# Case: one total order of a fused RWKV-7 and SwiGLU kernel exchanged for another

## The chip, the cores and the metric

One NeuronCore of a Trainium2 chip runs the whole program. The time is device microseconds of one execution; of the kernel before three runs are shown, and their median stands for it. Five engines work side by side, each through its own queue in order: TensorE (PE in the profile, its weight loads PEld), VectorE (DVE), ScalarE (ACT), GpSimd (POOL) and SyncE (SP), which only issues transfers. An engine waits for another one through semaphores. The profile shows one execution: the span from the first to the last instruction, what each engine did in it, and the clock that was granted to TensorE.

## The reference, cut to what matters

The first half is a recurrence over 768 time steps with one 40x40 state for each of 4 x 8 heads; its output, 3072 tokens of 320 numbers, goes through an RMS norm and a gated feed-forward block with 1536 hidden units. The weights arrive as 64-bit floats.

```python
for t in range(S):                                   # S = 768
    y[:, :, t] = np.einsum('bhd,bhde->bhe', rt, state)
    Sa = np.einsum('bhde,bhe->bhd', state, at)
    state_decay = state * wt[:, :, None, :] - np.einsum('bhd,bhe->bhde', Sa, bt)
    state = state_decay + np.einsum('bhd,bhe->bhde', vt, kt)
...
rms = np.sqrt(np.mean(x * x, axis=-1, keepdims=True) + 1e-06)
xn = x / rms * rms_g                                 # x: 3072 x 320
g = xn @ w_gate                                      # 320 x 1536
silu = g * (1.0 / (1.0 + np.exp(-g)))
val = xn @ w_val
return (silu * val @ w_out).astype(np.float32)
```

## The kernel before

**Tiling.** The 768 steps are cut into 24 chunks of 32. Within a chunk the recurrence is written as matrix products, so that only the state passes from chunk to chunk. A chunk c has three stages in the code:

- `front(c)` loads the chunk's inputs with transfers, mostly from GpSimd's queue (`wan`, `kbn`, `wn`, `VU`), turns them with TensorE transposes ("turn"), builds products of decays level by level (levels 1, 2, 4, 8, 16) and forms Gram products ("gramk", 32 small products a piece on 64-row tiles); VectorE puts their results under masks into `LT`, a triangular matrix for each head. Four transfers each then take `LT` through DRAM into another layout (`sB`, then `M`) on SP's queue.
- `inverse(c)` inverts those triangular matrices on VectorE, row by row (`Yi`, `tmp`), and sends the result back through DRAM (`sY`, then `LT`), again on SP's queue.
- `main(c)` carries the state forward: "state" and "lower" products, ScalarE's scaled copy `Xs`, a second "lower" (the solve, which reads the inverse that has landed in `LT`), ScalarE's copies into `VU`, "update" and VectorE's addition into `ST`. It then forms the outputs ("score", masks into `As`, "level" and "y0" products, sums into `y`), normalizes them (`ss`, `x`) and lays them, turned ("turn4", "turn3"), as 128-token columns into `xg`.

`feed(g)` is the feed-forward block for one or two chunks (13 groups, the first and the last with one chunk). It goes through the 12 slices of 128 hidden units two at a time: "h64" (products on half the rows) and "hh" (four full 128x128 products with 256 columns) into one PSUM room, ScalarE's SiLU into `sg`, VectorE's product into `hT`, and "out" (128x320 products) summed in `po` over all slices; at the end ScalarE copies `po` to `o` and four transfers on SP's queue store it. Around feed 0 `narrow` turns the 64-bit weights into 32-bit ones on VectorE and ScalarE.

A matrix product of the code is two products and two weight loads in TensorE's stream, a transpose is one of each; a piece of 16 small matrix products thus takes 64 instructions, a piece of 32 takes 128.

**What sets the order.** No loop order reaches the engines. Each call above adds a *piece* (one or more instructions of one engine) to a `Plan` with its needs; 5993 pieces in all (VectorE 2717, ScalarE 1113, TensorE 1091, GpSimd 588, SyncE 484). `Plan.issue` then walks the list `ORDER` and issues one piece per number. A number is the distance from the first piece that isn't issued yet, so the list is one total order, and each engine's queue is that order cut to its pieces. PSUM is given out the same way: `po` has one pair of banks, and three further pairs are shared by 495 *rooms*, short-lived buffers. A room's pair is its digit in `PAIRS`, and a room is entered only when the earlier one on that pair has been left. Between pieces of different engines that touch different banks or quadrants of a pair `issue` declares that there is no dependence; all others on a pair are kept apart by semaphores.

The list may also hold the word "-", which would issue a product on the identity that nothing uses (`plan.warm`, into a part of `po`). In the list of this kernel that word doesn't occur. `WARM` and `warm_until` are stored and not read on.

In the profile most instructions have the line of the helper that recorded them: L486 is any VectorE piece, L509, L513 and L516 ScalarE's activations, copies and scalings, L529 all transfers, L532 matrix products, L535 transposes. Groups are told apart by their tiles: `ps` is any room, `po<-wf,hT` an "out" product, `ps<-xg,wf` "h64" or "hh", `ps<-Xs,LT` the solve, `ps<-VU,KN` an update.

```python
i = first + int(word)          # in Plan.issue: the next piece
gone.add(i)
while first in gone:
    first += 1
...
nc.scalar.copy(po_[:, 0, DM:DM + P], plan.pairs[0][:, 0, 0:P])   # ahead of all pieces
```

Of the kernel before, what the change touches and what calls it, by code (L numbers as in the profile page):

```python
# [7 lines left out]
FP32 = mybir.dt.float32  # L8
# [8 lines left out]
P = 128  # L17
# [7 lines left out]
WARM = 230.0  # L25
# [232 lines left out]
class Plan:  # L258
# [82 lines left out]
    def issue(self, order, pairs):  # L341
# [6 lines left out]
        for word in order.split():  # L348
            if word == "-":
                self.order.append(None)  # L350
                self.warm()
                continue
# [759 lines left out]
```

## Time and profile before

| | us |
|---|---|
| runs shown | 1023.4, 1028.79, 1029.04 |
| median | 1028.79 |
| span of the profiled execution | 1017.9 |
| TensorE busy | 928.0 (91%), 24512 products |
| TensorE's weight loads busy | 754.3 (74%), 24512 loads |
| VectorE busy | 779.5 (77%) |
| ScalarE busy | 510.6 (50%) |
| GpSimd busy | 343.2 (34%) |
| mean granted clock of TensorE | 0.953 of full |

For the profiled execution only its span is given; what lies around the span is seen from the runs, which are 5.5 to 11.1 us longer. In the profile's slices a digit is the busy share of a fortieth of the span in tenths; PEclk is the clock in the same way. In the rows of stretches each engine has its busy time and, in brackets, its instructions; the last three columns are the granted clock, the transfers' share and GB/s. A wait is written as who waited, then for whom, with the sum, the times and the longest. In the timeline a row has start, duration, engine, line, what was written from what, and how many instructions in a row; the brackets tell how long the engine sat idle before it and what ended that. "issue" means that the profile shows nothing that it waited for.

### The profile page before, as it was taken

To read this page: it belongs to the slowest core of one execution; us is meant where nothing else is said; L and a number is where in the kernel's file an instruction comes from. 1 tells how busy PE (TensorE), PEld (TensorE's weight loads), DVE (VectorE), ACT (ScalarE), POOL (GpSimd) and SP (SyncE) were. 2 spreads that over 40 slices of the span, in tenths; PEclk is the share of its full clock that TensorE was granted. 3 is DMA by queue.
4 is the path that set the end of the run, shared out by engine and by line. 5 is a ranking of instruction groups with operands and counts; after the bars stand their busy time and mean duration, and the time that the engine had idled before them with its cause. 6 is when DMAs were issued, how large, how long until landed. Compare 5 with 4: busy or idle time off the path is not lost.

```text
span 1017.9 us, 55372 instructions
## 1 busy us (share of the span) xinstructions
PE 928.0 (91%) x24512; PEld 754.3 (74%) x24512; DVE 779.5 (77%) x2718; ACT 510.6 (50%) x1134; POOL 343.2 (34%) x595
## 2 busy tenths in 40 slices
PE   3457779998999999999999999999999999999998
PEld 3446668877777777787877778777787787787776
DVE  9989987786967976967868779669688788776531
ACT  6878656544454544454463444544535545435131
POOL 9966543313233233224321433224233323400000
PEclk9657768999999999999999999999999999999999
DMA  7764543313333223233231242232322422420100
GB/s 170 159 178 109 124 91 78 74 32 69 52 67 63 51 60 75 43 67 68 48 75 32 61 88 48 50 70 45 70 58 46 78 48 60 76 45 9 45 6 20
DMA packets 140175, 68.87 MB, mean 68 GB/s; under 512 B 120768, under 2 KB 127264, under 8 KB 139936
## 3 DMA queue, kind: packets, MB, share of 16 engines
q0 software_dynamic: 19680, 32.48, 15.8%
q1 hardware_dynamic: 118080, 32.54, 15.2%
q8 instruction: 192, 3.15, 1.3%
q10 hardware_dynamic: 2176, 0.33, 0.2%
q14 instruction: 47, 0.39, 0.1%
HBM read 55.05 MB, written 10.22 MB: 64 GB/s over the span
## 4 chain that ended last, share of the span: by engine, by line
PE 71%; DVE 12%; issue 5%; DMA 5%; ACT 3%; SPq 3%; DVEq 0%; ACTq 0%
PE ps L532 50%; PE po L532 14%; PE ps L535 6%; SPq L529 3%; DVE Yi L486 3%; DMA sY<-Yi 2%; DVE tmp L486 2%; DVE As L486 1%; DVE y L486 1%; ACT VU L513 1%; DVE LT L486 1%; DMA sB<-LT 1%; DVE K L486 1%; DVE wf L486 1%; DMA LT<-sY 1%
## 5 line engine op out<-in xcount | busy, mean ns | idle before, releaser
L532 PE MATMUL ps<-xg,wf 128*128 128x256 f32 (+3 forms) x1872 | 360.5, 374 | 2.4 <-issue 1.6
L532 PEld LDWEIGHTS ps<-xg,wf 128*128 128x128 f32 (+1 forms) x1872 | 267.5, 189 | 50.6 <-issue 14.5
L532 PE MATMUL po<-wf,hT 128*128 128x320 f32 x576 | 180.5, 447 | 0.5 <-issue 0.5
L486 DVE TENSOR_TENSOR hT<-ps,sg 128x256 f32<-128x256 f32 (+1 forms) x156 | 59.9, 399 | 95.3 <-PE ps L532 53.7
L532 PEld LDWEIGHTS po<-wf,hT 128*128 128x128 f32 x576 | 102.6, 189 | 37.8 <-issue 3.7
L486 DVE TENSOR_TENSOR tmp<-Yi,M 128x24 f32<-128x24 f32 (+21 forms) x512 | 107.3, 210 | 12.2 <-DMA M<-sB 1.4
L486 DVE TENSOR_TENSOR Yi<-Yi,tmp 128x24 f32<-128x24 f32 (+21 forms) x512 | 107.1, 209 | 11.1
L509 ACT ACTIVATE sg<-ps 128x256 f32<-128x256 f32 (+1 forms) x156 | 54.1, 368 | 116.9 <-PE ps L532 114.1
L529 POOL DMA_DIRECT2D VU<-in_v_dram x92 | 54.1, 590 | 145.7 <-PE ps L532 145.6
L486 DVE TENSOR_TENSOR K<-K,T 128x256 f32<-128x256 f32 (+1 forms) x191 | 91.9, 496 | 2.1 <-ACT T L513 0.7
L529 POOL DMA_DIRECT2D kbn<-in_k_dram x92 | 53.9, 588 | 101.3 <-PE ps L532 98.3
L519 POOL TENSOR_TENSOR ss<-ss,mhalf 128x1 f32<-128x1 f32 x24 | 14.4, 599 | 214.7 <-DVE ss L486 214.6
L532 PE MATMUL ps<-Ab,K 64*60 64x56 f32 (+2 forms) x4608 | 77.9, 223 | 7.3 <-issue 2.2
L532 PEld LDWEIGHTS ps<-Ab,K 64*60 64x60 f32 (+2 forms) x4608 | 71.2, 135 | 17.0 <-issue 10.3
L513 ACT COPY KN<-ps 128x640 f32<-128x640 f32 x95 | 65.1, 691 | 33.4 <-DVE LT L486 22.4
L529 POOL DMA_DIRECT2D kbn<-in_b_dram x92 | 54.1, 589 | 77.5 <-PE ps L532 76.3
L486 DVE TENSOR_TENSOR As<-ps,msi 128x256 f32<-128x256 f32 (+1 forms) x168 | 70.5, 455 | 10.6 <-PE ps L532 6.4
L532 PEld LDWEIGHTS ps<-As,KN 128*40 128x40 f32 x3072 | 67.2, 128 | 12.9 <-issue 7.4
L532 PE MATMUL ps<-As,KN 128*40 128x32 f32 x3072 | 72.1, 208 | 4.2 <-issue 2.7
L513 ACT COPY K<-K 128x512 f32<-128x512 f32 x95 | 60.3, 635 | 23.5 <-PE ps L532 12.0
L486 DVE SCALAR_TENSOR_TENSOR Yi<-M,Yi 128x31 f32<-128x31 f32 (+6 forms) x228 | 44.7, 244 | 33.5 <-DMA M<-sB 17.1
L529 POOL DMA_DIRECT2D wn<-in_w_dram x92 | 52.1, 568 | 19.6 <-DVE KN L486 18.5
(138 smaller groups left out, 1525.4 us busy)
## 6 DMA issues: line engine op xcount, KB each, us to landing
M<-sB SPq DMA_DIRECT2D x96, 128.0 KB, 3.0
wan<-in_r_dram SPq DMA_DIRECT2D x24, 160.0 KB, 4.0
kbn<-in_b_dram POOLq DMA_DIRECT2D x92, 40.0 KB, 2.6
kbn<-in_k_dram POOLq DMA_DIRECT2D x92, 40.0 KB, 2.8
VU<-in_v_dram POOLq DMA_DIRECT2D x92, 40.0 KB, 2.8
wan<-in_a_dram POOLq DMA_DIRECT2D x46, 80.0 KB, 2.9
wan<-in_w_dram POOLq DMA_DIRECT2D x46, 80.0 KB, 3.0
wn<-in_w_dram POOLq DMA_DIRECT2D x92, 40.0 KB, 2.5
```

Source lines behind the costliest of these rows:

```text
L486: plan.add("DVE", time + more + each * size(o), 0.087, lambda at: [fn(at(o), *m(at))], [o], aps(*args))
L509: scalar(o, [a], lambda at: nc.scalar.activation(at(o), at(a), f, **kw), aps(acc), 0.1 if f in (AF.Square, AF.Relu) else 0.0)
L513: scalar(o, [a], lambda at: nc.scalar.copy(at(o), at(a)), extra=more)
L519: plan.add("POOL", 0.5, 0.06, lambda at: nc.gpsimd.tensor_tensor(o, a, b, op), [o], [a, b])
L529: plan.add(by, 0.6 if by == "POOL" else 0.45, 0.0, lambda at: queue.dma_start(out=o, in_=i), [o], [i], load=load, since=since)
L532: return o, lhsT, rhs, lambda at: nc.tensor.matmul(at(o), lhsT, rhs, start=start, stop=stop, skip_group_check=True), 4
L535: return o, i, ident, lambda at: nc.tensor.transpose(at(o), i, ident), 2
```

## The change

The list `ORDER` and the digits `PAIRS` are replaced. The pieces, their instructions and their operands are the same; the new list has 5993 numbers and 495 digits as well. With it go `WARM`, `warm_until`, the word "-" and `plan.warm`, which the old list didn't use, and the copy into `po` at the start that prepared the bank for it. In `Plan.add` the rule goes that a room's first piece also had to follow whatever the room's later pieces need; it only constrained the list and issues nothing.

The lists are cut here to their first and last lines.

```diff
--- before.py
+++ after.py
@@ -22,7 +22,6 @@
 S0, S1 = 15.0, 2.0
 LEAD = 2
 BLOCKED = 5
-WARM = 230.0
 
 
 
@@ -31,216 +30,164 @@
 
 
 ORDER = """
-73 389 194 84 48 2 74 55 86 388 3 202 192 693 0 202 35 3 63 4 24 5 46 74 82 0 51 199 78 75 74 64 65 69 362 0 360 42
...
-103 107 109 99 100 104 105 110 114 115 111 116 2 0 0 0 1 0 0 0
+83 82 72 81 64 2 25 4 3 51 191 86 193 74 73 71 5 6 7 8 46 55 75 388 9 10 11 0 27 388 0 58 387 64 38 0 17 366 39 72
...
+0 3 18 10 25 29 30 2 20 31 14 4 5 19 26 13 0 0 10 4 0 0 10 0 10 0 0 0 0 1 3 2 0
 """
 
 PAIRS = """
-01201022112022100110102011022020010212121202001021010102112022021121000002012011202021202100112210021101221101111021
...
-0000212011200201122120202010201
+120121001120102110210211010112001212102010120110200101221101102001010022201020212012211110202122121012120200221102012120
...
+010012112210012
 """
 
 
@@ -259,19 +206,18 @@
 
 
 
-    def __init__(self, pairs, stand_ins, warm_until):
+    def __init__(self, pairs, stand_ins):
         self.pieces, self.seen, self.masks = [], {}, {}
         self.pairs, self.stand_ins = pairs, {t.tensor.name: t for t in stand_ins}
         self.now = {n: None for n in self.stand_ins}
         self.rooms = []
         self.stage, self.count = ("", 0), {}
-        self.warm_until = warm_until
 
     def room(self):
 
         name = list(self.stand_ins)[len(self.rooms) % len(self.stand_ins)]
         self.now[name] = len(self.rooms)
-        self.rooms.append([0, None, None])
+        self.rooms.append([0, None])
         return self.stand_ins[name]
 
     def foot(self, ap):
@@ -330,11 +276,6 @@
             self.pieces[i].users.append(me)
         if piece.room is not None:
             room = self.rooms[piece.room]
-            room[2] = first = me if room[2] is None else room[2]
-            for i in needs:
-                if i < first and first not in self.pieces[i].users:
-                    self.pieces[i].users.append(first)
-                    self.pieces[first].missing += 1
             room[0] += 1
         self.pieces.append(piece)
 
@@ -346,10 +287,6 @@
             room[1] = int(pair)
         held = [None] * len(self.pairs)
         for word in order.split():
-            if word == "-":
-                self.order.append(None)
-                self.warm()
-                continue
             i = first + int(word)
             gone.add(i)
             while first in gone:
@@ -471,7 +408,7 @@
 
 
     plan = Plan([psum.tile([P, 2, 512], FP32, name=f"ps{i}") for i in range(3)],
-                [dram.tile([P, 2, 512], FP32, name=f"room{i}") for i in range(8)], WARM)
+                [dram.tile([P, 2, 512], FP32, name=f"room{i}") for i in range(8)])
 
     def size(ap):
         n = 1
@@ -559,7 +496,6 @@
     nc.vector.memset(plan.pairs[0], 0.0)
     for t in plan.pairs[1:]:
         nc.scalar.copy(t, plan.pairs[0])
-    nc.scalar.copy(po_[:, 0, DM:DM + P], plan.pairs[0][:, 0, 0:P])
 
     eye = const.tile([P, C // 4, C], FP32, name="eye")
     iw = eye[:, 0:3].bitcast(I32)
@@ -1075,7 +1011,6 @@
             front(c + 2)
             inverse(c + 2)
 
-    plan.warm = lambda: nc.tensor.matmul(po_[:, 0, DM:DM + P], ident, ident, start=False, stop=False, skip_group_check=True)
     plan.tc = tc
     with tc.manual_schedule():
         plan.issue(ORDER, PAIRS)
```

More of the change, by code (lines that the diff above doesn't have):

```diff
@@ L24 @@
 BLOCKED = 5
-WARM = 230.0
 EPS = 1e-6
 ORDER = """
[202 rows of a table removed]
[150 rows of a table added]
 """
 PAIRS = """
-01201022112022100110102011022020010212121202001021010102112022021121000002012011202021202100112210021101221101111021
-21221111212100211220100022221222210112000202222102022010002011120122201200200022220201022020211100121210011101212110
-01102212121112121022202222101111222021011121120020201102120220002012010200121012011112212020021020210202102101220221
-20222210212101010200002012100221211100002021212100100110101002022010122212112021000222212011011102000102021222022121
-0000212011200201122120202010201
+120121001120102110210211010112001212102010120110200101221101102001010022201020212012211110202122121012120200221102012120
+211111012201100102221010120111022010100220222221122220210100012120110122222221010100100012011202020112010101001022010101
+011101101010222221211121011010000120121211022201112120202120101000102121010110212202012222210012120122221120202012021100
+121212200120120111101010222012010010112121121202202121212020202200020010201211112020210100122202000001010210222021002010
+010012112210012
 """
```

348 rows, old and new, of the table ORDER are left out of this document.

## The prediction

> **What bounds the kernel now.** I read the page's slices first, then stretches of time, then what TensorE (PE) waits for, then single instants.
>
> ```profile
> PE   3457779998999999999999999999999999999998
> ...
> DVE  9989987786967976967868779669688788776531
> ...
> PEclk9657768999999999999999999999999999999999
> ...
> q8 instruction: 192, 3.15, 1.3%
> ```
>
> PE is nearly full from the eighth slice on and the granted clock is full from there; before that VectorE (DVE) is the full engine and the clock alternates. The last line is the queue that brings instructions: 192 packets, 3.15 MB. The border between the two phases is the first product of feed 0, at 163.7 us, and PE's last product ends at 1013.4. Busy time by stretch (columns PE, PEld, DVE, ACT, POOL; then clock):
>
> ```profile
> 0.00:163.70 163.70, 100.55 (x3876) 90.33 (x3876) 147.11 (x435) 117.79 (x229) 115.45 (x208) 0.71 0.58 135
> 163.70:200.00 36.30, 34.36 (x971) 30.35 (x966) 28.07 (x98) 19.28 (x46) 8.23 (x14) 1.00 0.37 73
> 200.00:950.00 750.00, 729.85 (x18965) 582.94 (x18953) 581.36 (x2101) 359.02 (x820) 218.95 (x373) 1.00 0.29 58
> 950.00:1013.40 63.40, 63.29 (x726) 50.67 (x725) 22.99 (x86) 14.10 (x41) 0.56 (x1) 1.00 0.06 11
> 1013.40:1018.00 4.60, 0.00 (x0) 0.00 (x0) 0.00 (x0) 0.40 (x1) 0.00 (x0) 1.00 0.14 36
> ```
>
> In the start DVE idles 163.7 - 147.1 = 16.6 us. In the main phase PE is busy 34.4 + 729.9 + 63.3 = 827.5 of 849.7 us: only 22.2 us are idle, so an order can win there from idle time or from products that run shorter. What that idle time ends on, in the same phase:
>
> ```profile
> PE ps L532 <- issue: 14.4, 19, 1.7
> PE ps L535 <- issue: 1.4, 2, 1.2
> PE ps L535 <- DVE hT L486: 1.2, 2, 0.8
> PE ps L532 <- DMA LT<-sY: 1.1, 2, 0.8
> ```
>
> 16.3 us (with 0.5 of `po`) end on "issue", which is no engine and no transfer; 5.9 are left for all engines and DMAs. Two such instants in the timeline:
>
> ```profile
> 234.90 0.64 PE L532 MATMUL ps<-VU,KN 64*40 64x40 f32 x47
> 237.24 0.38 PE L532 MATMUL ps<-VU,KN 64*40 64x40 f32 x17 [1.70 <-issue]
> ...
> 567.15 0.26 PE L532 MATMUL ps<-Xs,LT 32*32 32x40 f32 x5
> ...
> 568.79 0.76 PE L532 MATMUL ps<-Xs,LT 32*32 32x40 f32 x59 [1.38 <-issue]
> ```
>
> Both halts fall inside one piece of 64 equal products, where nothing new is needed. They have a grid. PE's stream has 24512 loads, 24512 products and 272 waits; 3.15 MB over these is 64 bytes each, so a packet of 16 KB is 256 instructions. Numbering all of them in time, 24 of the 39 gaps over 0.36 us in the main phase stand at number 193 modulo 256 exactly, among them ten of the twelve over 1 us. They sum to 22.2 us from start to start (part of this the page counts as busy, since a product's modelled end reaches into the gap). So PE outruns its instruction packets where 256 instructions are short: a "lower" piece (64 small products, 128 instructions) takes 0.72 us. Two packets never start closer than 3.29 us, and each takes 0.9 to 1.5 us.
>
> The Trainium skill, "Runtime: NRT & Kernel Launch", section "Instruction fetch mechanics", agrees on the 256 instructions of a block, but calls crossing a block mostly hidden and gives PE room for 2048 instructions. The trace differs: a halt at the same place of the grid, up to 1.9 us from start to start. By the page, the second term of the sum below would be zero.
>
> **The change, part by part.** Both lists hold the same 5993 pieces; decoded, 747 of PE's 1091 pieces get another predecessor, moved by one place in the median and 19 at most; DVE's by two. PE works off a like amount per DVE work all along (at 300 us of DVE work, 261 us of PE work before and 265 after, by mean durations). So it is a local reshuffle.
>
> *Idle products.* Neither list has the word that issues one, so nothing goes. What goes is one ScalarE copy into `po`, 0.27 us at 4.81. Behind it stands ScalarE's own transfer at 4.92, and PE's first product starts at 8.10 on a VectorE `eye` wait: taken as 0; -0.3 if that cover is gone.
>
> *Switches between tile sizes.* A feed piece on the full array ("hh": four 128x256 products; "out": four 128x320) costs, from its start to the next piece's, 0.86 between two full ones, 0.96 ahead of a small-tile piece, 0.97 after one and 1.06 between two; "out" 1.08, 1.17, 1.18, 1.28 (medians of the main phase). Entering costs 0.10, leaving 0.10. The old list enters full tiles 180 times, the new one 166: 14 x 0.20 = **-2.8 us**, all of it on PE in the main phase.
>
> *Instruction packets.* I laid both lists on the grid of 256 (four instructions a product of the code, two a transpose; 57 waits ahead of feed 0, the rest spread evenly), gave each piece the lower quartile of its kind and neighbours, and summed for every 256 instructions what is missing to 3.2 us, a little under the closest two packets. Old: 35 short stretches, 24.5 us; the trace has 22.2. New: 19, 15.2 us. In the trace's measure (15.2 - 24.5) x 22.2/24.5 = **-8.4 us**. With 3.0 or 3.4 in place of 3.2 it is -7.6 or -8.9. The weak point is where the waits fall in the new list. With the grid moved by 16 instructions to the late side it gives 22.3 (-2.0), by 48 30.9 (+5.8), by 8 to the early side 14.3 (-9.2). I take -8.4, since the even spread also reproduced the old list (24.5, against 23.6 with its true waits).
>
> *Waits of PE for engines.* A feed room's last product and the next room's first on the same bank pair have 2.05 us of PE work between them in the median (2.27 before) and 0.99 at the tenth percentile (1.17); "hh" and its "out" 9.6 (7.3). One hand-over in ten of 73 loses up to 0.18, +1.3; all of the 5.9 may go: -5.9. I take 0, the two tendencies being opposite.
>
> *The start.* Ahead of feed 0, DVE's work is 145.4 us before and 145.8 after, PE's pieces the same (58.6 us at full clock): 0. Bounds: -16.6, all of DVE's idle time; +3.4, one full-clock stretch of 6.8 us more at half rate (in the trace full-clock stretches of the start last 3.4 or 6.8).
>
> *DMA queues.* SP's and GpSimd's issues move too, by 2.8 and 8.1 places in the mean. The output transfers of a feed stand up to 35 places earlier on SP, right after their copy; behind each are the transfers of the triangular inverse (`sB`, `M`, `sY`, `LT`). SP already waits 93.6 us on that copy without PE showing it. What PE could feel is `LT`, which "lower" number two (the solve) reads: the trace has its landing 2.5 us after issue in the median, 4.5 at most, and 5.6 us in the median between the last issue and the solve. In the new list 3.3 us of PE work lie there. While a landing stays below that it is free: 0; the far end is the second rival.
>
> *Tail.* Feed 12 still ends on its "out" products, then 4.6 us of copy and transfer: 0.
>
> Sum: -2.8 - 8.4 = -11.2 on the profiled execution, whose span is 1017.9: 1006.7. The median of the three runs shown is 10.9 above that span (they run from 5.5 to 11.1 above); so 1028.8 - 11.2 = **1017.6, said as 1018**, 1.0% less.
>
> **Rivals.** *The halts stay.* The waits fall otherwise in the new stream, or the halts come from something else than packets; then the switches alone remain: 1028.8 - 2.8 = 1026. For it: the other 15 gaps, 9.1 us in sum, lie off the grid; the sum swings by 7 us within 16 instructions. Against: the exact grid in 24 cases, and that the new list is lowest just where the trace's grid lies. Halved, the second term gives 1022. The Trainium skill's "mostly hidden" (same page and section) would give the 1026 too. Both are "no change".
>
> *The solve waits for its inverse.* The new list places `LT`'s last issue 3.3 us ahead of the solve in 22 chunks (3.0 or less in nine). It decides from the point where landings take longer than 3.3: at the 4.5 that the trace shows at most, each solve is 1.2 short, 22 x 1.2 = +26, and 1028.8 - 11.2 + 26 = 1044: slower. For it: SP's queue is in order, so an output transfer that waits for its copy holds all behind it. Against: median landing 2.5, and PE lost just 1.1 us on `LT` so far.
>
> *It does not do what it says:* "idle products left out" removes none, shown above; priced in the sum.
>
> **Chances and range.** Under 1% either way can hardly be told from no change here, since the three runs lie 5.6 us apart; the bounds are 1018.5 and 1039.1. My sum lies right at the first: 0.46 that it comes out whole or better (idle on engines or in the start falling too, down to 1028.8 - 11.2 - 5.9 - some of the 16.6, near 1005); 0.41 for the halved and lost second term, 1019 to 1030 or a little above; 0.13 for the solve. Leaving out the far end of either side, the range is 1005 to 1034.
>
> **What would show it.** In the changed kernel's profile: 192 packets again; gaps at one place of the 256-grid summing to about 14 us, in some 15 to 20 places; PE idle in the main phase near 14 us instead of 22; feed 0 at 162 to 167 us; "hh" and "out" rows a little shorter in the mean; `PE <- DMA LT<-sY` still under 3 us. Wrong would be: issue waits as long as before (first rival), long waits of "lower" on `LT` (second), or feed 0 far from 164, which my zero for the start denies.

## The result, and the profile after

The changed kernel is **slower** by 1.1%: 1039.82 us in the median of 12 runs against 1029.62 for the kernel before, ratio 1.011 (95% interval 1.007 to 1.015; the two medians alone give 1.010). The forecast was 1018. Ratios leave out runs more than 1.5% above the fastest of their kernel: none of these, but three of e5_oldstart's twelve below, whose 1.002 is 1.005 with all of them.

The profiled execution of the changed kernel took 1038.29 us, its span is 1036.5: what lies around the span is 1.8 us. The execution of before that the prediction worked from (span 1017.9) was therefore some 10 us faster than its kernel's median, and faster than each of the twelve runs: of the 5.5 to 11.1 us given ahead of the prediction for what lies around its span, 1.8 do, and the rest is how fast that one execution was. So the two traces lie 18.6 us apart where the medians lie 10.2 apart.

The slices of the changed kernel (busy tenths; PEclk is the granted clock):

```profile
PE   4457668999999999999999999999999989999998
...
DVE  8988877876967976966968779768679768665631
...
PEclk9556767999999999999999999999999999999999
```

PE fills up as late as before, and VectorE (DVE) has lost a little in the first eight slices. The border is in the stretches (columns PE, PEld, DVE, ACT, POOL, then clock):

```profile
0.00:174.00 174.00, 104.13 (x3876) 93.81 (x3876) 146.19 (x437) 116.69 (x227) 116.49 (x210) 0.68 0.57 129
174.00:200.00 26.00, 25.33 (x721) 22.27 (x717) 22.62 (x84) 15.34 (x35) 4.73 (x9) 1.00 0.23 50
200.00:950.00 750.00, 724.02 (x18839) 582.48 (x18828) 569.23 (x2086) 357.75 (x819) 221.06 (x376) 1.00 0.30 58
950.00:1032.00 82.00, 80.18 (x1102) 64.11 (x1100) 31.98 (x114) 19.13 (x54) 0.55 (x1) 0.98 0.10 21
```

The first product of feed 0 comes at 174.0 us instead of 163.7, with the same VectorE work (146.2 us against 147.1) and so 27.8 us of VectorE idle instead of 16.6. The main phase, from there to PE's last product, takes 857.9 us instead of 849.6, and PE idles 28.4 us in it instead of 22.2. PE's waits in the main phase:

```profile
PE ps L469 <- issue: 11.7, 11, 2.1
PE ps L469 <- DMA LT<-sY: 4.7, 7, 2.5
PE ps L469 <- DVE hT L423: 3.4, 5, 1.3
PE ps L469 <- ACT sg L446: 1.7, 2, 1.2
PE ps L472 <- issue: 1.5, 1, 1.5
PE ps L472 <- DMA wan<-in_r_dram: 1.2, 1, 1.2
```

"issue" fell from 16.3 to 13.2 us; engines and transfers rose. Measured as the prediction measured it (start to start, over 0.365 us, with all of PE's instructions numbered):

| main phase, us | before | after | difference |
|---|---|---|---|
| PE's pieces at the traces' prices (worked out), switches included | 803.2 | 799.5 | -3.7 |
| gaps at number 193 modulo 256 ("on the grid") | 22.2 (24) | 15.7 (12) | -6.6 |
| all other gaps | 9.1 (15) | 27.1 (40) | +18.0 |
| the rest | | | +0.6 |
| feed 0 to last product | 849.6 | 857.9 | +8.3 |

So the halts on the grid shrank, and that was paid back twice over by gaps off the grid. By what ended them, these are: VectorE's `hT` 7.5 us (10 gaps; before 2.2), the landing of `LT` 7.1 (8; before 1.5), and 4.4 us (9 gaps) that are no waits but products at half clock. One place of slowed products, in four windows of 3.41 us, and PE's instructions in the second and third:

```profile
719.67:723.09 3.42, 3.42 (x78) 2.77 (x77) 3.25 (x11) 2.02 (x6) 0.09 (x1) 1.00 0.24 41
723.09:726.50 3.41, 1.93 (x80) 1.62 (x76) 1.28 (x4) 0.97 (x2) 0.00 (x0) 1.00 0.16 27
726.50:729.91 3.41, 3.41 (x8) 1.99 (x6) 1.82 (x4) 2.02 (x6) 1.24 (x2) 0.50 0.25 43
729.91:733.33 3.42, 3.35 (x159) 2.69 (x158) 0.00 (x0) 1.62 (x6) 0.00 (x0) 1.00 0.61 158
```

```profile
724.01 0.38 PE L472 MATMUL ps<-ident,y 40*128 40x40 f32 x5
725.87 0.31 PE L472 MATMUL ps<-ident,y 40*128 40x40 f32 x3 [1.48 <-issue]
726.12 4.11 PE L469 MATMUL po<-wf,hT 128*128 128x320 f32 x8
```

PE was busy for 1.93 of 3.41 us in the second window; in the third the granted clock is 0.50, and eight "out" products fill it. The halt that emptied the second window stands inside one piece, at number 193: it is one of the halts on the grid (1.71 us from start to start). The main phase has one more such window, at 955.2 us, and it too follows a halt at number 193 (1.82 us at 954.7; PE busy for 1.67 of 3.42 us). So the slowed products belong to the grid, and not to other engines: against full clock the two windows cost up to 1.7 us each, and the gaps behind engines and transfers grew by 18.0 - 4.4 = 13.6 us. The trace of before has 24 halts of up to 1.90 us and no window at half clock in its main phase.

### The profile page after: what moved, and what is told of

Its sections match the earlier page's. It is cut to its first block, busy times and chain, and to the rows that moved or that the text cites. A ratio compares the mean times of both kernels' runs of the same rounds, so it can differ in the third digit from the quotient of the medians.

```text
span 1036.5 us, 55370 instructions
## 1 busy us (share of the span) xinstructions
PE 933.7 (90%) x24512; PEld 762.7 (74%) x24512; DVE 770.0 (74%) x2718; ACT 509.3 (49%) x1133; POOL 342.8 (33%) x595
## 3 DMA queue, kind: packets, MB, share of 16 engines
q0 software_dynamic: 19680, 32.48, 15.3%
## 4 chain that ended last, share of the span: by engine, by line
PE 59%; DVE 16%; DMA 9%; SPq 5%; issue 5%; ACT 4%; POOL 1%; DVEq 0%; ACTq 0%; POOLq 0%
PE ps L469 42%; PE po L469 12%; SPq L466 5%; PE ps L472 5%; DVE Yi L423 4%; DVE tmp L423 3%; DMA LT<-sY 3%; DMA M<-sB 2%; DVE y L423 2%; DVE LT L423 1%; DMA sB<-LT 1%; DVE As L423 1%; DMA sY<-Yi 1%; DVE hT L423 1%; DVE K L423 1%
## 5 line engine op out<-in xcount | busy, mean ns | idle before, releaser
L469 PEld LDWEIGHTS po<-wf,hT 128*128 128x128 f32 x576 | 105.2, 191 | 35.4 <-issue 1.0
L469 PE MATMUL ps<-Ab,K 64*60 64x56 f32 (+2 forms) x4608 | 82.2, 226 | 15.3 <-issue 5.6
L469 PEld LDWEIGHTS ps<-Ab,K 64*60 64x60 f32 (+2 forms) x4608 | 74.2, 137 | 26.6 <-issue 10.5
L450 ACT COPY KN<-ps 128x640 f32<-128x640 f32 x95 | 65.4, 692 | 47.8 <-DVE LT L423 30.9
L450 ACT COPY K<-K 128x512 f32<-128x512 f32 x95 | 60.2, 634 | 21.9 <-DVE K L423 9.2
L456 POOL TENSOR_TENSOR ss<-ss,mhalf 128x1 f32<-128x1 f32 x24 | 15.3, 638 | 146.4 <-DVE ss L423 146.3
```

Of the source, the lines that this page charges most:

```text
L450: scalar(o, [a], lambda at: nc.scalar.copy(at(o), at(a)), extra=more)
L456: plan.add("POOL", 0.5, 0.06, lambda at: nc.gpsimd.tensor_tensor(o, a, b, op), [o], [a, b])
L469: return o, lhsT, rhs, lambda at: nc.tensor.matmul(at(o), lhsT, rhs, start=start, stop=stop, skip_group_check=True), 4
```

## The experiments

Each ratio is to the kernel before, with its 95% interval. "Main" is feed 0 to the last product, "on" and "off" are the gaps on and off the grid, "half" the windows at half clock in the main phase, all from one profile each.

| run | ratio | feed 0 | main | on | off | half |
|---|---|---|---|---|---|---|
| before | 1 | 163.7 | 849.6 | 22.2 | 9.1 | 0 |
| changed kernel | 1.011 (1.007-1.015) | 174.0 | 857.9 | 15.7 | 27.1 | 2 |
| e1_oldlist | 1.001 (0.998-1.004) | 167.9 | 851.9 | 20.1 | 12.8 | 0 |
| e1_oldstart | 1.017 (1.013-1.021) | 179.2 | 860.7 | 18.0 | 28.6 | 3 |
| e1_newstart | 1.001 (0.998-1.004) | 171.1 | 853.4 | 19.7 | 18.8 | 3 |
| e1_earlylt | 1.021 (1.016-1.025) | 175.2 | 871.1 | 18.3 | 38.3 | 7 |
| e2_ss | 1.008 (1.006-1.011) | 172.1 | 857.3 | 15.3 | 25.7 | 2 |
| e2_dve | 1.103 (1.099-1.107) | 174.8 | 953.5 | 8.1 | 134.9 | 14 |
| e2_queues | 1.123 (1.119-1.128) | 175.4 | 979.1 | 14.0 | 162.3 | 16 |
| e2_grid48 | 1.017 (1.012-1.022) | 171.7 | 865.0 | 26.9 | 25.4 | 2 |
| e3_queues | 0.996 (0.993-0.999) | 171.2 | 840.5 | 9.5 | 19.2 | 0 |
| e3_dve | 1.002 (0.998-1.005) | 172.8 | 851.2 | 13.1 | 21.9 | 0 |
| e3_oldqueues | 1.002 (0.998-1.005) | 171.7 | 851.2 | 21.3 | 14.2 | 2 |
| e4_queues | 0.995 (0.992-0.999) | 170.1 | 838.5 | 8.9 | 17.4 | 1 |
| e5_oldstart | 1.002 (0.999-1.006) | 168.0 | 853.1 | 17.2 | 18.6 | 0 |
| e5_newstart | 1.003 (1.000-1.005) | 174.9 | 846.9 | 19.8 | 8.4 | 0 |
| e5_best | 0.990 (0.985-0.994) | 163.7 | 842.4 | 15.4 | 14.2 | 1 |

All edits are to `ORDER` and `PAIRS` alone, except where said; a diff of the numbers tells nothing, so the diffs below are of an engine's queue, one piece a line (stage, chunk, what it writes, its number in the stage).

**e1_oldlist**, the control: the old list and digits in the new code.

```diff
 ORDER = """
-83 82 72 81 64 2 25 4 3 51 191 86 193 74 73 71 5 6 7 8 46 55 75 388 9 10 11 0 27 388 0 58 387 64 38 0 17 366 39 72
+73 389 194 84 48 2 74 55 86 388 3 202 192 693 0 202 35 3 63 4 24 5 46 74 82 0 51 199 78 75 74 64 65 69 362 0 360 42
...
```

> The list and the room digits of before in the changed kernel's code, so only the copy into po at the start and the unused word are gone. Both theories: the same time as before, ratio 0.995 to 1.005, feed 0 at 161 to 167 us in the profile, VectorE idle ahead of it 15 to 19 us, some 24 gaps at one place of the 256-grid. If feed 0 comes at 172 or later here, the copy, and not the order, made the start longer.

It is the kernel before, within 0.4%. The copy into `po` is worth nothing that can be told; feed 0 came at 167.9 with the same start as in the 163.7 of the first profile, so 4 us there are one execution's chance.

**e1_oldstart and e1_newstart**, two splices at feed 0's first product. The pieces up to there come in one list's order, the rest in the other's.

```diff
 the list
-1054 pieces as in the new list, 4939 as in the new list
+1058 pieces as in the old list, 4935 as in the new list     (e1_oldstart)
+1054 pieces as in the new list, 4939 as in the old list     (e1_newstart)
```

> The first 1058 pieces as the list of before issues them, up to feed 0's first product; all other pieces in the sequence of the new list. Theory 'two losses': the start is back at 163 to 166 us, the main phase keeps what the new list has there (857.9 us from feed 0 to the last product, against 849.6), so the profiled span is 1021 to 1029 and the ratio to before 1.004 to 1.009. Rival 'one loss, handed on': the late start of feed 0 is what the main phase stumbled over (transfers and VectorE work that come late); with the old start the main phase falls below 849.6 too, since it has 6.6 us less of halts at the grid and 3.7 us less of work: span 1007 to 1012, ratio 0.99.

> The first 1054 pieces as the new list issues them, up to feed 0's first product; all others in the sequence of the list of before. Theory 'two losses': feed 0 at 171 to 176 us, main phase 847 to 852 us, span 1023 to 1031, ratio 1.007 to 1.011. Rival 'a lucky clock': the ten microseconds of the start come from where the full and the half clock fell in that one execution, not from the order; then feed 0 comes at 162 to 168 us in the profile and the ratio is 0.997 to 1.003.

Neither theory foresaw the first: the old start made it worse (1.017), and feed 0 came at 179.2. The second is level with before, as "a lucky clock" had the ratio, but with feed 0 at 171.1, as "two losses" had it. The digits had been taken from the list of the main phase, as far as they fitted, with pairs 1 and 2 exchanged in name: of the start's 67 rooms, e1_oldstart has 57 on the pair that the new list gives them and 20 on that of before (no renaming of the pairs makes it more than 32). So these two splices mix order and digits; e5 sorts that out.

**e1_earlylt**, the prediction's second rival. SP's queue alone, for the inverse's transfers; chunk 16 as an example:

```diff
+inverse 15: LT1 (67)
+inverse 15: LT1 (64)
+inverse 15: LT1 (65)
 front 16: sB0 (72)
+inverse 15: LT1 (66)
 front 16: sB0 (74)
 front 16: sB0 (71)
 front 16: sB0 (73)
-inverse 15: LT1 (67)
-inverse 15: LT1 (64)
-inverse 15: LT1 (65)
-inverse 15: LT1 (66)
 front 16: M0 (75)
```

> The new list; only the transfers of the triangular inverse on SP's queue (sY, LT) stand up to 3 us of TensorE work earlier, none ahead of what it needs; every other engine's queue is the same. Theory 'the solve waits for its inverse': PE's waits on LT in the main phase fall from 4.7 to under 1.5 us, off-grid gaps from 27 to 21 or less, the time by 3 to 6 us (ratio to before 1.005 to 1.008 instead of 1.011). Rival 'lateness moves on': the solve gets its LT, but PE then waits at the next hand-over (hT, VectorE being held by M's landing), and the time stays within 2 us of the changed kernel's (ratio 1.009 to 1.013).

The gaps behind `LT` did go, and the kernel became 1% slower still. What happened in that chunk, first SP's queue, then VectorE's:

```profile
652.08 1.32 SPq L503 DMA_DIRECT2D LT<-sY  x3
653.50 0.40 SPq L503 DMA_DIRECT2D sB<-LT  x1
653.93 1.15 SPq L503 DMA_DIRECT2D LT<-sY  x1
655.12 1.45 SPq L503 DMA_DIRECT2D sB<-LT  x3
660.61 3.48 SPq L503 DMA_DIRECT2D M<-sB  x4
```

```profile
656.32 0.15 DVE L460 TENSOR_SCALAR ss<-ss 128x1 f32<-128x1 f32 x1 [0.62 <-ACT x L483]
666.72 1.45 DVE L460 SCALAR_TENSOR_TENSOR Yi<-M,Yi 128x31 f32<-128x31 f32 x7 [10.25 <-DMA M<-sB]
```

`sB`'s operand was ready at 651.8. Now its transfers stood behind and between `LT`'s, which waited for `sY` to land, so `M` landed late and VectorE, whose next piece needs `M`, stood still for 10.25 us with pieces that PE needed behind it. PE then idled 4.96 us at 670.7, and two windows at half clock followed. The rival "lateness moves on" holds, and its price was put too low.

**e2_ss**, GpSimd's queue alone: seven small normalization pieces ahead of a transfer that waits for another engine.

```diff
 front 16: kbn1 (12)
+main 13: ss1 (45)
 front 16: wn0 (19)
-main 13: ss1 (45)
 front 15: VU1 (7)
```

> The new list; on GpSimd's queue alone seven of the small normalization pieces (ss) stand 2.4 places earlier in the mean, ahead of transfers that wait for TensorE; all other queues are the same. In the changed kernel these pieces start 10.4 us in sum after their operand is there (4.7 at 527 us the longest), in the kernel before 4.5. Theory 'a short piece behind a waiting transfer': that sum falls to under 4, PE's waits behind ScalarE's x and sg fall by 2 to 4 us, and the ratio to before from 1.011 to 1.005 to 1.009. Rival 'no part of it': 1.009 to 1.013, off-grid gaps 25 us or more as in the changed kernel (27.1).

The lateness of `ss` fell from 10.4 to 2.8 us in sum, PE's waits on `x` and `sg` from 2.0 to 0.7, and the ratio from 1.011 to 1.008. The two intervals overlap and the gaps off the grid fell by just 1.4 us, to 25.7 (the rival had 25 or more): in the direction of the theory, not proven.

**e2_dve and e2_queues**, the two largest misses. TensorE's order and the digits stay; from feed 0 on VectorE's queue (e2_dve) or all four others (e2_queues) are put in the order that a replay found best. The replay lets every engine work off its queue in order with the traces' median durations, starts a piece when its needs have ended, and keeps a move of one piece when PE's last product comes earlier.

```diff
 inverse 12: tmp0 (42)
-front 13: T1 (35)
 inverse 12: Yi0 (43)
+main 11: y0 (40)
 inverse 12: tmp1 (44)
 inverse 12: Yi0 (45)
-front 13: A0 (27)
 inverse 12: tmp0 (46)
```

> The new list with VectorE's queue alone in another order from feed 0 on (1911 of its 2717 pieces, by 3 places in the mean: masks As 4 earlier, hT 2 earlier, the inverse's Yi and tmp a little later); PE, ScalarE, GpSimd and SP have the same queues. Theory 'VectorE is held behind the landing of M': PE's waits on hT fall from 7.5 us in gaps to under 4, off-grid gaps from 27 to 16 to 22, ratio to before 1.002 to 1.007. Rival 'the loss sits in TensorE's order': VectorE's queue makes no difference, ratio 1.009 to 1.013.

> The new list's order of TensorE and its room digits; from feed 0 on the queues of VectorE, ScalarE, GpSimd and SP are put in another order (1921, 728, 366 and 315 pieces, by 2 to 4 places in the mean). Theory 'the hand-overs are the loss': with TensorE's order as it is, off-grid gaps fall from 27.1 us to 8 to 15, the gain at the grid and at the switches stays (grid gaps 13 to 20, pieces 799.5 us), so from feed 0 to the last product 838 to 846 us instead of 857.9, and the ratio to before is 0.988 to 1.000. Rival 'the loss sits in TensorE's order' (rooms taken in turns leave the next engine too little time): off-grid gaps stay above 20 us and the ratio at 1.006 or more.

They were 10 and 12% slower, far beyond what either pair of theories had in mind (the second meets its rival by the letter): the replay was wrong. Two things were missing in it, and the traces show both. First ScalarE's waits in the main phase of e2_dve, then of the changed kernel:

```profile
ACT As L490 <- DVE As L460: 64.5, 25, 6.2
```

```profile
ACT As L453 <- DVE As L423: 16.7, 12, 4.0
```

Neither reads what the other writes: both read the same room, and engines take turns at a bank, in the list's order. In the main phase of the changed kernel the starts on PE, VectorE and ScalarE that come 0.4 us or more after all that a piece needs (its operands, and the piece ahead in its own queue) sum to 46 us, in e2_dve to 153; once earlier pieces at the same bank and quadrant are counted as needs, 2 and 8 remain. The kernel before has 52 and 3: turns at a bank made e2_dve slow, but they do not tell the changed kernel from before. (The Trainium skill, "PSUM — Partial Sum Buffer", section "PSUM bank collisions raise a hardware error", says that two engines must not be at one bank and quadrant at once, readers included, and that a dependency is put between them; the traces agree.)

Second, VectorE runs a piece that doesn't need its predecessor 0.082 us *before* the predecessor's end (median of some 1600 neighbours in the changed kernel's main phase), and one that does 0.035 us after it (674 neighbours). The search had pulled the independent pieces out from between the inverse's `tmp` and `Yi`: dependent neighbours rose from 674 to 1085, and 411 x 0.117 = 48 us of VectorE time with them.

**e2_grid48**, the packets. Twelve products on the identity in PE's idle places of the start, used by nothing, as the old code's word "-" would issue them: 48 instructions.

```diff
+            if word == "-":
+                self.warm()
+                continue
...
+    nc.scalar.copy(po_[:, 0, DM:DM + P], plan.pairs[0][:, 0, 0:P])
...
+    plan.warm = lambda: nc.tensor.matmul(po_[:, 0, DM:DM + P], ident, ident, start=False, stop=False, skip_group_check=True)
```

> The new list with twelve products on the identity between TensorE's pieces of the start (each where TensorE idled 1.5 to 6 us in the changed kernel), 48 instructions more in its stream, so that the 256-instruction grid lies 48 later in the list from feed 0 on. Nothing uses these products; all queues are else the same. Theory 'instruction packets': the halts stay at number 193 modulo 256 of the longer stream, fall on other products, and sum to 24 to 30 us instead of 15.7, the time rises by 5 to 13 us over the changed kernel's (ratio to before 1.016 to 1.024). Rival 'a place in the program': the halts come before the same products as in the changed kernel, at number 241, and sum to 14 to 17; ratio 1.008 to 1.013.

As the packets would have it: 25 gaps at number 193 modulo 256 of the longer stream, 26.9 us, and one gap of 0.4 us at 241. The same 64 products of an update, with the 48 instructions and in the changed kernel:

```profile
365.09 0.72 PE L510 MATMUL ps<-VU,KN 64*40 64x40 f32 x54
367.85 0.31 PE L510 MATMUL ps<-VU,KN 64*40 64x40 f32 x10 [2.03 <-issue]
```

```profile
361.10 0.81 PE L469 MATMUL ps<-VU,KN 64*40 64x40 f32 x64
```

The main phase is 7.1 us longer and the ratio 1.017, with an interval that overlaps the changed kernel's: where the grid falls is worth 11 us of halts in this kernel, by these two profiles.

**e3_queues, e3_dve, e3_oldqueues**: the same search with a replay that knows the turns at a bank and the two spacings. Fed with the orders run so far, it gives, by its own working and not by a run, main phases of 12 us (changed kernel), 25 (e1_earlylt), 93 (e2_dve) and 107 (e2_queues) above that of before; the chip had shown 8, 22, 104 and 130. VectorE's queue as an example (e3_dve):

```diff
 inverse 13: Yi0 (17)
+front 13: T1 (70)
+feed 5: hT0 (26)
+feed 5: hT0 (31)
 inverse 13: tmp1 (18)
```

> The new list's order of TensorE and its room digits; from feed 0 on the queues of VectorE, ScalarE, GpSimd and SP in another order again (1739, 697, 367 and 307 pieces, by 2 to 4 places in the mean), now chosen by a replay of the traces' rows that knows two things the runs before showed: engines that touch one PSUM bank wait for each other in the list's order, and VectorE starts a piece 0.08 us before the end of one it doesn't need but 0.035 after the end of one it needs (674 such neighbours in the changed kernel, 1085 in the run that was a tenth slower, 600 to 640 here). Theory 'the hand-overs are the loss': by the replay PE waits 27 us less than in the changed kernel, half of it real: off-grid gaps from 27.1 to 8 to 16 us, main phase 835 to 848 instead of 857.9, ratio to before 0.984 to 0.998. Rival 'the loss sits in TensorE's order': off-grid gaps above 20, ratio 1.005 or more.

> The new list with VectorE's queue alone in another order from feed 0 on, chosen by the same replay (1767 pieces, by 2.3 places in the mean); the other four queues as in the changed kernel. Theory 'VectorE is the late engine': it wins some half of what all four queues win: off-grid gaps 14 to 21 us, ratio to before 0.995 to 1.004. Rival 'ScalarE and GpSimd are late' (normalization and bank turns): nothing gained, 1.008 to 1.013.

> The list of before with its order of TensorE and its digits; from feed 0 on the other four queues in another order, chosen by the same replay (1708, 702, 360 and 302 pieces). The replay finds 14 us less of PE's waits, against 27 for the new list. Theory 'hand-overs': off-grid gaps from 9 to 13 us down to 3 to 7, ratio 0.991 to 0.998, behind the new list's re-placed queues by what the grid (22.2 against 15.7 us) and the switches (3.7 us) are worth, 3 to 10 us. Rival 'before is at its floor': 0.998 to 1.003.

With TensorE's order and the digits untouched, the other queues alone turn 1.011 into **0.996**: main phase 840.5 us instead of 857.9. So the new order of TensorE does not have to lose; what the other queues make of it decides. That the loss was PE's waiting for them is shown in part only. Of the 17.4 us, 6.2 are halts on the grid, 4.4 the products at half clock (none in this profile), 3.3 stand in no gap over 0.365 us, and 3.5 are the gaps behind engines and transfers: these fell from 22.7 to 19.2 us, where the theory had 8 to 16 off the grid (`hT` from 7.5 to 4.3; `LT` stayed, 7.1 and 7.6). The halts moved although TensorE's order did not: its stream has 11 waits less ahead of its 10660th product (115 against 126), and waits count for the grid. How much of the gain comes that way, and so by chance, was not separated.

VectorE's queue by itself brings the ratio to 1.002, and the main phase to 851.2: the search moved pieces that PE waits for (`As` 1.7 places, `K` 1.8, `hT` 0.6, in the mean of those that moved) ahead of the inverse's, which are needed only at the solve. But the gaps behind engines and transfers hardly fell (22.7 to 21.9); the halts fell by 2.6 us and the products at half clock (4.4) are gone, so that VectorE is the late engine is not shown by it. It is not VectorE's time behind `M`, which I had first taken for the cause; these two rows are of the changed kernel (1.011) and of e3_dve (1.002), VectorE's waits in the main phase:

```profile
DVE Yi L423 <- DMA M<-sB: 38.0, 11, 6.3
```

```profile
DVE Yi L460 <- DMA M<-sB: 48.8, 13, 6.0
```

More of that wait, and a faster kernel. The old list gains nothing by the same search (1.002), as the rival has it, and its 21.3 us on the grid stay; that no other order of its queues does better is not shown by one search.

**e4_queues**: the search once more, with longer landings.

> As the re-placed queues before it (TensorE's order and the room digits of the new list, ratio 0.996), but the replay now counts a landing of LT as 3.9 us from its issue, of M as 4.3 and of sY as 3.2, where it had 2.7, 3.9 and 2.5: in ten traces, where a solve waited for LT it started 3.0 to 6.7 us after the issue, 4.35 in the median. Theory 'the solve waits for its inverse' as far as it is left: PE's gaps behind LT fall from 7.6 us to under 3, off-grid gaps from 19.2 to 10 to 15, main phase 833 to 839 us instead of 840.5, ratio to before 0.988 to 0.996. Rival 'landings scatter too much to be planned for': LT gaps stay above 5 us or others take their place, ratio 0.994 to 0.999.

```diff
 landings in the replay, us from issue
-LT 2.7, M 3.9, sY 2.5
+LT 3.9, M 4.3, sY 3.2
```

The rival holds for `LT`: the gaps behind it are still 7.1 us in eight places, and the ratio (0.995) can't be told from e3's. Of the theory's other marks the main phase (838.5) came and the gaps off the grid (17.4, not 10 to 15) did not. The gaps behind `hT` are down to 1.0 us, from 7.5 in the changed kernel. PE's largest waits in its main phase, where `LT` is by far the largest beside "issue":

```profile
PE ps L513 <- issue: 5.4, 7, 1.5
PE ps L513 <- DMA LT<-sY: 5.3, 8, 1.2
PE ps L516 <- issue: 1.1, 1, 1.1
```

**e5_oldstart, e5_newstart, e5_best**: clean splices, each room of the start with its own list's digit.

```diff
 PAIRS, first 67 rooms / other 428
-20 / 427 as in the list they come from, pairs 1 and 2 exchanged in name   (e1_oldstart)
+67 / 428                                   (e5_oldstart; e5_newstart and e5_best likewise)
```

> The first 1058 pieces as before issues them, with the digits that before gives their 67 rooms; all other pieces and the other 428 rooms as in the new list. (In the splice before this one the start's rooms had mostly the new list's digits: 32 of 67 as before, and feed 0 came at 179 us.) Theory 'the start costs nothing in the median': feed 0 at 163 to 172 us, main phase 855 to 861, ratio 1.007 to 1.013 as the changed kernel. Rival 'the start is worth its ten microseconds': ratio 0.999 to 1.005. If feed 0 comes at 177 or later again, the digits were not what made it late.

> The first 1054 pieces and their 67 rooms' digits as in the new list, all others, with their digits, as before. Theory 'the start costs nothing in the median': ratio 0.998 to 1.003, feed 0 at 168 to 174 us in the profile. Rival 'it costs ten': 1.006 to 1.011.

> The first 1058 pieces and their rooms' digits as before; from there on the re-placed queues with the new list's order of TensorE (ratio 0.995 with the new list's start, main phase 838.5 us). Theory 'the start costs nothing': 0.992 to 0.998. Rival 'the old start is worth some microseconds': 0.985 to 0.991, and this is the fastest of all.

e5_oldstart and e1_oldstart issue the very same pieces in the very same order; what differs is the bank pair of 47 of the start's 67 rooms and of one later room (beside the exchange of names, which is taken to cost nothing). It is worth 1.1 to 1.4% (1.017 against 1.005 with all runs, or 1.002): feed 0 at 168.0 instead of 179.2, in one profile each. How that also reached the main phase (853.1 against 860.7, where three windows at half clock fell) is not settled.

The parts add up to less than the whole: new start alone +0.26%, new main phase alone +0.24% (+0.5 with all runs of e5_oldstart), both +1.1%. The intervals allow it (the two together up to +1.1, both at once at least +0.7), and the gaps behind `LT` scatter from one execution of the same main phase to the next (7.1, 6.1, 3.7 and 1.9 us in four profiles, one of them e2_ss). Better told is the start by its profiles: feed 0 at 163.7 to 171.7 in five with the old start and digits (mean 167.0), at 170.1 to 175.4 in nine with the new (173.4). And e5_best is **0.990** (0.985 to 0.994), where the same main phase behind the new start had 0.995 (0.992 to 0.999): by these the old start is worth some 6 us, though the intervals touch. It beats both kernels. Its stretches:

```profile
0.00:163.70 163.70, 98.36 (x3878) 88.12 (x3878) 146.40 (x435) 117.74 (x228) 115.05 (x207) 0.73 0.58 135
163.70:1006.10 842.40, 822.47 (x20638) 665.35 (x20636) 617.36 (x2283) 392.93 (x905) 229.06 (x389) 1.00 0.28 55
```

## Why the prediction was wrong

**Switches between tile sizes (-2.8): counted right, not seen by itself.** The -3.7 us of the table are the two lists at the traces' prices, and no measured sum. The sign that was named, shorter "hh" and "out" rows, can't be told: 374 to 375 and 447 to 446 ns a product, where 2.8 us are about 1 ns on each of the 2448.

**Instruction packets (-8.4): right in mechanism, too large in effect.** 192 packets again; the gaps at number 193 fell by 6.6 us to 15.7 (forecast about 14), in 12 places instead of the 15 to 20 named. But a halt can cost more than its length: the two windows at half clock behind halts gave back up to 3.4 us in this execution, and the prediction has no such price. The step that could be moved at will was moved by e2_grid48: the halts stood at number 193 again and summed to 26.9 us, against 30.9 x 22.2/24.5 = 28.0 by the count. The "mostly hidden" of the Trainium skill ("Runtime: NRT & Kernel Launch", section "Instruction fetch mechanics"), weighed there, does not hold for this kernel, and with it goes the first rival.

**Waits of PE for engines (0, bounds -5.9 to +1.3): this step failed.** The gaps behind engines and transfers grew by 13.6 us, of which `LT` is 5.6, `hT` 5.3 and single waits (`sg`, `wan`, `KN`, `x`) the rest; against e1_oldlist, a more usual execution of before, they grew by 9.9. I had bounded it by one kind of hand-over alone, the next room on the same bank pair, measured in PE's work, and set "the two tendencies" against each other. PE's work between two pieces says nothing on whether the other engine's queue has come that far. What stands ahead of `hT`, `As` or `K` in VectorE's own queue, and of `sg` in ScalarE's, the prediction never laid out; that it matters is seen in e4_queues, where the other queues alone took the gaps behind `hT` from 7.5 to 1.0 us. That these places explain the whole 13.6 us is not shown: e3_queues and e4_queues still have 19.2 and 15.9 us of such gaps, and before 9.1.

**The start (0, bounds -16.6 to +3.4): this step failed too.** "The same work" is not "the same time": with equal work on VectorE and PE the new start takes 6.4 us more in the mean of the profiles (10.3 in the pair compared), beyond the upper bound. The bank digits, which I didn't price at all, move it by 11 us with the order held (one profile each, where executions of one start lie up to 8 us apart). PE's waits ahead of feed 0 in the changed kernel (up to 174 us):

```profile
PE ps L472 <- ACT exs L446: 7.6, 2, 3.8
PE ps L469 <- DMA LT<-sY: 7.0, 2, 6.4
```

The first row is of ScalarE's narrowing of the weights (`exs`, 0.7 us a piece), which now stands ahead of copies that PE's transposes need: 4.9 to 17.2 us in nine profiles with the new start, 0 to 2.1 in five with the old one. The second row does not tell them apart (6.9 us before). That the first makes up the 6 us was not tested by itself.

**DMA queues (0) and the second rival.** The solve did wait more for `LT`: 1.5 us before, 1.9 to 7.1 in four profiles of the new main phase. It was neither nothing nor the 26 us of the rival, presumably since covers of 3.3 us of PE's work are longer in time as soon as PE idles anywhere. That rival's 1044 came nearest to the 1039.8 by luck: `LT` cost 5.6 of its 26 us.

**The offset.** I took the difference of the traces over to the median of the runs, which is sound; but the one profile was faster than all twelve runs, and feed 0 alone moves by 8 us between executions of the same start.

**What hid the mistake** is that the two terms with a price were gains, both counted in the stream of one engine, and that what had no row was set to zero. The priced terms sum to -10.3 in the table, near the -11.2, before the half clock behind the halts; of the zeros, the idle products (e1_oldlist) and the tail (4.6 us again) held, and the waits, the start and `LT` were losses.

## What to carry to other kernels

When an order is exchanged, lay out for each engine what stands ahead of the pieces that the bound engine waits for: work between two pieces of the bound engine is no cover if the other engine's queue is late. Split a gain by kind before it is called the proof of a cause: here most of what re-placed queues won stood at the grid and in the clock. Before trusting a replay, let it reproduce a kernel that is known to be bad; here it needed the turns at a PSUM bank and the spacing of dependent neighbours before it ranked orders as the chip did, and then it found one that beats both lists. A long order file has more in it than its order: digits of banks in the start were worth about 1%, and 48 instructions' shift of the stream 0.6%.

## What the hardware showed

**The clock goes by fixed windows, and half a window is enough.** In 17 profiles the granted clock changes only on a raster of 3.413 us, at another offset in every execution. A window at full clock in which PE was busy under 45% was followed by half clock in 101 of 103 cases, with 45 to 60% in 66 of 148, with 60 to 70% in 5 of 123, above 70% in none of 4105. Out of half clock, no window under 80% led back (329 cases), and 126 of 144 above 95% did. The Trainium skill, "TensorE: Matmul & The Clock Gate", section "HAM oscillation — how this bites in real kernels", has a rule of no idle gaps over some 3.4 us; here an idle of 1.48 us inside one window (57% busy) already halved the next, so the rule is too mild. As the raster starts anywhere, the same stall can cost nothing in one execution and up to 1.7 us in the next; that this is part of the scatter of the runs is likely, not shown.

**VectorE overlaps neighbours, but not dependent ones:** 0.117 us for each pair, 0.035 after against 0.082 before the predecessor's end.

**Landings scatter.** Where a gap of PE ended on `LT` (70 in 17 profiles), the solve started 1.9 to 5.6 us after the issue, 4.4 in the median; VectorE's pieces that waited for `M` 2.6 to 5.2 (5th to 95th percentile of 171).
